# A planner of instruction order with new costs for the opening, new landing times and a new table of noises

## The chip, the cores and the metric

The kernel runs on one core of one Trainium2 chip. The metric is the device time of one execution in microseconds (us). Before the change the median of three runs is 1648.17 us (1646.45 to 1650.07).

## What is computed

The reference has two parts. For each of 8 batches and 8 heads, with 576 positions of 64 elements in float32:

```
kv  = k^T v                      # 64 x 64 per head
out = q kv                       # 576 x 64 per head
x   = out / sqrt(mean(out^2) + 1e-6) * g_norm
```

The heads of a batch are laid side by side, which gives x as 4608 rows of 512. Then four experts, each with weights w1 (512 x 1024) and w2 (1024 x 512):

```
p    = domain_probs / sum(domain_probs)
out += p[:, e] * (relu(x @ w1[e]) @ w2[e])    # for e = 0..3
```

## The kernel before

**Tiling and stages.** x is kept transposed and cut into 9 chunks of 512 rows (the first 512 positions of each batch, and a ninth of what is left over). A step is one expert on one chunk, so there are 36 steps, expert by expert. A step forms the products of x with w1 (`up`), applies relu, and forms the products with w2 (`down` or `down_deep`), one step later. Most products are made by a scheme of seven products of quarter blocks in place of eight, nested twice, so that sums and differences of blocks (`combine`, L549, on DVE or POOL) and evacuations of PSUM (L1417 and L1745 on ACT, L1425 and L1753 on DVE) run beside PE all the time. PE's products of both stages have the line of one helper, L526.

**The opening** (`opening`, from L845) treats batch 0, four pairs of heads. For each pair SP issues the loads of q, k and v (L555). PE turns q (L875, evacuated by ACT, L880), forms keys times values and turns the rest of q (L890, L894), and ACT and DVE copy the result (L909, L906). Two attention products follow (L929), into two halves (`raw`) of shared PSUM banks. Their squares (L805, ACT), sums (L812, DVE), roots (L772) and inverses (L779 to L784), and the scaling (L824, DVE) give x, which PE turns again (L949) and ACT evacuates (L955). Then the first products with w1 (`up_plain`, L526) can run. The remainder of batch 0 is L969 and L983. While PE has nothing to do in the opening, the planner inserts filler products on the identity (L1906).

**The other batches** (`attention`, from L1005) come one per step in steps 0 to 6: q is loaded in eight pieces and transposed by DVE (L1050); products at L1077, L1102, L1144; roots go by DRAM (L1180, L1189, L1196).

**At the expert changes** (steps 8, 17 and 26 on) `weights_1` and `weights_2` load the next weights. Differences with weights that are in DRAM are made by `subtract_from`: ACT writes the negated copy (L622), then POOL issues a load that adds to it (L628). Results of expert 0 go out by SP (L1592), later ones by POOL with addition (L1590), those of the very last step by SP again.

**What sets the order.** The order of the instructions of all five queues is written out when the kernel is built. Each operation is added to a `Plan` with a key (its place in the stream of steps), a cost per engine, and for transfers its size `kb` and the time `lands` from issue to landing. `prepare` gives each a due time: the summed PE cost ahead of its key, lowered so that what depends on it can be on time. `run` then steps through time, and each free engine begins the operation with the earliest due time among those that it takes to be ready (`ready`, `delay`); SP takes the first in order of key. `begin` books the end: for SP a bus of 215 KB per us before `OPEN` = 36 us and 260 after, with at least `lands` after that; for POOL's transfers a bus of 130. Each engine executes its queue in the order so found, and waits for what is really late. `deal` moves the due times of the operations of a step (and of the next) by a pseudorandom noise; the table `DEALS` says which noise each step gets.

The choice in `run` and the landing in `begin`:

```
best = op
if eng in self.FIRST or eng == "PE" and t < self.OPEN:
    break
...
self.bus = max(self.bus, t + 1.5) + op.kb / (215.0 if t < self.OPEN else self.RATE)
op.end = self.bus + 0.5
if t >= self.OPEN:
    op.end = max(op.end, t + op.lands)
```

Of the kernel before, what the change touches and what calls it, by code (L numbers as in the profile page):

```python
# [41 lines left out]
class Plan:  # L42
# [25 lines left out]
    DEALS = {  # L68
        -2: 8, -1: 32, 0: 171, 1: 147, 2: 82, 3: 196, 4: 105, 5: 75, 6: 79, 7: 39, 8: 54, 9: 73, 10: 115,
        11: 84, 12: 12, 13: 6, 14: 6, 16: 1, 17: 3, 18: 10, 19: 11, 20: 2, 21: 1, 22: 4, 23: 4, 25: 5, 26:  # L70
        8, 27: 6, 33: 3, 34: 4
# [33 lines left out]
    def prepare(self, slots, later, idle, idle_banks, idle_until):  # L105
# [49 lines left out]
        self.bus, self.port, self.held, self.bus_pool = 3.8, 0.0, None, 0.0  # L155
# [11 lines left out]
    @staticmethod  # L167
    def noise(*key):

        def mix(x):  # L170
            x = (x ^ x >> 16) * 0x7feb352d & 0xffffffff
            x = (x ^ x >> 15) * 0x846ca68b & 0xffffffff
            return x ^ x >> 16

        n, step, i = key
        x = mix(n * 2654435761 + (step + 8) * 40503 & 0xffffffff)
        x = mix(x + i * 2246822519 & 0xffffffff)
        y = mix(x + 1 & 0xffffffff)
# [3 lines left out]
    def deal(self, step, n):  # L182

        k = len(self.SPREADS)
        wide = self.SPREADS[n % k] if n else 0.0
        wide_pe = self.SPREADS_PE[n // k % len(self.SPREADS_PE)] if n else 0.0
        for op in self.steps[step] + self.steps.get(step + 1, []):
            z = wide_pe if "PE" in op.cost else wide
            op.due = op.base + (z * self.noise(n, step, op.n) if z else 0.0)

    def layout(self, *how):

        self.prepare(*how)
        for step in sorted(self.steps):
            self.deal(step, self.DEALS.get(step, 0))
# [17 lines left out]
    def delay(self, d, eng):  # L213

        if self.t < self.OPEN:
            return 0.06 if d.eng == eng else 0.2
# [8 lines left out]
    def ready(self, op, eng, front):  # L225
# [34 lines left out]
    def run(self, until):  # L260
# [3 lines left out]
        while self.left:  # L264
# [6 lines left out]
            for eng in todo:  # L271
# [10 lines left out]
                for op in pending:  # L282
# [19 lines left out]
                    if eng in self.FIRST or eng == "PE" and t < self.OPEN:  # L302
                        break
# [27 lines left out]
    def begin(self, op, eng):  # L331
        t, wake, free = self.t, self.wake, self.free
        op.start, op.eng = t, eng
        if eng == "SP":
# [3 lines left out]
            if t >= self.OPEN:  # L338
                op.end = max(op.end, t + op.lands)
            self.lanes = self.lanes[1:] + [op.end]  # L340
        else:
            op.end = t + op.cost[eng]
            self.busy[eng] = op.end - (self.OVERLAP[eng] if t >= self.OPEN else 0.0)
            if op.kb:
                self.bus_pool = max(self.bus_pool, op.end + 2.0) + op.kb / self.RATE_POOL
                op.end = max(op.end + op.lands, self.bus_pool)
        if eng == "PE":
            self.worked += op.cost[eng]
        if op.port:
# [20 lines left out]
        for b in op.bufs:  # L370
            b.left -= 1
            if b.left == 0 and b.kind is not None:
                early = t < self.OPEN
                end = max(
                    o.end + (0.2 if early else self.AFTER_PE if o.eng == "PE" else self.FREED)
# [12 lines left out]
        if t < self.OPEN:  # L388
            heapq.heappush(wake, op.end + 0.06)
            heapq.heappush(wake, op.end + 0.2)  # L390
# [11 lines left out]
def kernel(  # L402
# [150 lines left out]
    def load(key, buf, dst, src, kb, reads=(), also=(), lands=4.0, issue=0.55):  # L553
# [64 lines left out]
    def subtract_from(key, to, view, a, src, reads, writes):  # L618
# [10 lines left out]
            reads=[to], writes=writes, kb=512, lands=6.0,  # L629
        )  # L630

    def weights_1(e, key, step, need):
# [4 lines left out]
        for i, (n, dh, uh) in enumerate(((1, 0, 0), (2, 1, 0), (21, 0, 1), (4, 1, 1))):  # L637
# [5 lines left out]
                w1_src(e, dh, uh), 512 if e else 300, also=[corner[n]], lands=6.0,  # L643
# [48 lines left out]
    def weights_2(e, key, step, deep):  # L692
# [3 lines left out]
        for i, (n, uh, dh) in enumerate(((1, 0, 0), (2, 1, 0), (12, 0, 1), (3, 1, 1))):  # L696
# [4 lines left out]
                w2_src(e, uh, dh), 512 if e else 330, also=[corner[n]], lands=6.0,  # L701
# [67 lines left out]
    def inverse_root(key, ss, rt, n, count):  # L769
# [17 lines left out]
        plan.add(key - 0.3, {"ACT": 0.2}, root, reads=[ss], writes=[rt])  # L787
        plan.add(key - 0.3, {"DVE": 0.75}, invert, reads=[ss, rt], writes=[ss, rt], port=True)
# [56 lines left out]
    def opening(key, span, rem):  # L845
# [11 lines left out]
        for hp in range(NPAIR):  # L857
            n = f"{b}_{hp}"
            loaded = {}
            for t, src, kb in (("q", q, 172), ("k", k, 172), ("v", v, 172)):  # L860
# [16 lines left out]
            plan.add(at(hp), {"PE": 0.44}, turns, reads=[qt], writes=[bank])  # L877
# [22 lines left out]
            for other in range(2):  # L900
                to, at_ = (kv_own, kv_other)[other], slice(other * D, (other + 1) * D)
                for r in range(2):
                    c = r ^ other
                    plan.add(
                        at(hp), {"DVE": 0.235} if r else {"ACT": 0.24},
# [17 lines left out]
            def attend(eng, raw=raw, kv=kv, qT=qT, other=0, wide=wide):  # L923
# [12 lines left out]
                at(hp + 0.4), {"PE": 0.36 if wide == D else 0.5}, attend, reads=[qT, kv_own], holds=[kv], writes=[raw])  # L936
            plan.add(
                at(hp + 0.4), {"PE": 0.36 if wide == D else 0.5}, lambda eng, attend=attend: attend(eng, other=1),
# [12 lines left out]
            plan.add(at(hp + 1), pe(4, P, 1), turn_x, reads=[x], writes=[bank])  # L951
# [13 lines left out]
        def attend_rem(eng):  # L965
# [9 lines left out]
            at(NPAIR), {"PE": 0.9}, attend_rem,  # L975
# [29 lines left out]
    def attention(b, key, span, rem):  # L1005
# [26 lines left out]
        for s in range(2):  # L1032
# [3 lines left out]
            for r in range(2):  # L1036
                for dh in range(2):
                    for o in range(2):
# [6 lines left out]
                                "(n p) d -> p n d", p=R), 170 if b == 1 else 118,  # L1045
# [475 lines left out]
    def result(s, e, c, base):  # L1521
# [60 lines left out]
        def send(key, i):  # L1582
# [4 lines left out]
            def fn(eng):  # L1587
# [9 lines left out]
                lands=5.6 if e and not again else 4.5,  # L1597
# [245 lines left out]
    plan.add(-1.99, {"PE": 0.3}, turn_gains, reads=[gain_row], writes=[gain_bank])  # L1843
# [117 lines left out]
```

## Time and profile before

| | |
|---|---|
| median of three runs | 1648.17 us |
| the profiled execution | 1651.69 us |
| its span, first to last instruction | 1649.9 us |
| PE busy, share of the span | 1632.6 us, 99% |
| DVE, ACT, POOL busy | 1316.6, 972.8, 620.5 us |
| granted TensorE clock, mean | 0.999 |
| DMA over the span | 240.97 MB, mean 146 GB/s |

The profile shows one execution. Rows of the time line give the start and the busy us, engine, line, operation, tiles written and read, and how many instructions were merged into the row; the brackets hold the time that the engine was idle before it, and what released it. Lines are those of the kernel before. A matmul in float32 is two instructions in the counts. SPq and POOLq are the queues' own work of issuing transfers. `big`, `u`, `db`, `ab` and so on are kinds of buffers; the last three are banks of PSUM.

### The profile page before, as it was taken

What the parts mean: (1) busy time and instruction counts of PE and PEld (TensorE: products, weight loads), DVE (VectorE), ACT (ScalarE), POOL (GpSimd) and SP (SyncE); (2) the same over time, 40 slices, a digit from 0 to 9 for tenths busy, and PEclk for the clock granted to TensorE, in tenths of its full rate; (3) what the DMA queues carried; (4) which work ended last, traced back from release to release, by engine and by line L of the source; (5) the groups of instructions that cost most, each with busy time, mean ns of one, the idle gap of its engine ahead of it and who ended that gap; (6) DMA issues with size and microseconds to landing.
All of it is one profiled execution on the core that took longest, in us unless ns stands there. A gap on an engine that the chain in (4) does not pass through costs nothing.

```text
span 1649.9 us, 66218 instructions
## 1 busy us (share of the span) xinstructions
PE 1632.6 (99%) x28724; PEld 1554.8 (94%) x28724; DVE 1316.6 (80%) x2188; ACT 972.8 (59%) x2462; POOL 620.5 (38%) x641
## 2 busy tenths in 40 slices
PE   9999999999999999999999999999999999999998
PEld 6688789888999999999999999999999999999997
DVE  5777887878888878788887898777898887778776
ACT  3455554655656666666656666655666566666653
POOL 4132323232433453443344443333344444442333
PEclk9999999999999999999999999999999999999999
DMA  9977886654764435444566444444578444444432
GB/s 230 215 172 206 228 227 174 152 194 175 219 170 130 117 92 155 117 112 109 168 158 167 115 106 119 114 117 113 135 186 187 117 117 117 107 115 116 117 104 53
DMA packets 225597, 240.97 MB, mean 146 GB/s; under 512 B 100890, under 2 KB 165274, under 8 KB 225306
## 3 DMA queue, kind: packets, MB, share of 16 engines
q1 hardware_dynamic: 201690, 199.96, 40.0%
q0 software_dynamic: 23616, 36.78, 14.8%
q8 instruction: 225, 3.69, 0.9%
q14 instruction: 66, 0.54, 0.1%
HBM read 162.21 MB, written 74.47 MB: 143 GB/s over the span
## 4 chain that ended last, share of the span: by engine, by line
PE 92%; DMA 4%; SPq 2%; DVE 1%; issue 1%; ACT 0%; POOL 0%; DVEq 0%; POOLq 0%; ACTq 0%
PE u L526 45%; PE db L526 29%; PE ab L526 15%; DMA out_dram<-big 1%; SPq L555 1%; PE ab L1077 1%; DMA big<-in_moe_w_dram 1%; DMA kv<-in_v_dram 1%; PE ab L1102 1%; DVE big L549 0%; PE ab L1144 0%; DMA big<-roots 0%; PE db L1102 0%; PE ab L1906 0%; PE u L890 0%
## 5 line engine op out<-in xcount | busy, mean ns | idle before, releaser
L549 DVE TENSOR_TENSOR big<-big,big 128x1024 f32<-128x1024 f32 (+1 forms) x539 | 502.0, 946 | 44.8 <-ACT big L1381 18.0
L526 PE MATMUL u<-xf,big 128*64 128x128 f32 x6496 | 476.0, 273 | 0.3
L526 PE MATMUL db<-big,big 128*64 128x128 f32 (+1 forms) x5552 | 425.7, 290 | 1.5 <-ACT big L1745 0.9
L526 PE MATMUL u<-xf,w1y 128*64 128x128 f32 x5304 | 396.5, 273 | 3.8 <-ACT u L1417 2.4
L526 PEld LDWEIGHTS u<-xf,big 128*64 128x64 f32 x6496 | 382.4, 137 | 5.1 <-ACT snap L1417 1.4
L526 PEld LDWEIGHTS db<-big,big 128*64 128x64 f32 x5552 | 332.1, 137 | 28.9 <-ACT big L1745 1.4
L526 PEld LDWEIGHTS u<-xf,w1y 128*64 128x64 f32 x5304 | 314.1, 137 | 8.1 <-ACT u L1417 2.6
L1425 DVE TENSOR_TENSOR big<-u,snap 128x256 f32<-128x256 f32 x448 | 188.3, 421 | 121.2 <-PE u L526 83.7
L1417 ACT ACTIVATE snap<-u 128x256 f32<-128x256 f32 x490 | 187.9, 384 | 148.7 <-PE u L526 130.3
L549 POOL TENSOR_TENSOR big<-big,big 128x256 f32<-128x256 f32 (+1 forms) x145 | 152.7, 1055 | 219.2 <-DVE big L549 111.3
L1417 ACT ACTIVATE big<-u 128x256 f32<-128x256 f32 x448 | 171.1, 385 | 86.9 <-PE u L526 68.0
L549 POOL TENSOR_TENSOR big<-big 128x512 f32<-128x512 f32 (+1 forms) x89 | 107.3, 1207 | 250.7 <-DVE big L549 115.6
L1745 ACT ACTIVATE snap<-db 128x256 f32<-128x256 f32 (+1 forms) x256 | 90.4, 353 | 122.8 <-PE db L526 100.7
L1381 ACT ACTIVATE big<-big 128x1024 f32<-128x1024 f32 x127 | 133.7, 1054 | 12.3 <-DVE big L549 11.2
L1753 DVE TENSOR_TENSOR big<-ab,snap 128x256 f32<-128x256 f32 x174 | 73.2, 421 | 64.4 <-ACT snap L1745 42.6
L1590 POOL DMA_DIRECT2D out_dram<-big x122 | 106.7, 1233 | 31.9 <-ACT big L1566 24.2
L1417 ACT ACTIVATE u<-u 128x256 f32<-128x256 f32 x245 | 90.8, 371 | 37.6 <-PE u L526 25.1
L549 DVE TENSOR_TENSOR big<-big 128x512 f32<-128x512 f32 (+1 forms) x145 | 109.0, 755 | 1.6 <-ACT big L1381 1.5
L526 PE MATMUL ab<-kv,big 128*64 128x128 f32 x1416 | 99.6, 273 | 0.0
L1566 ACT ACTIVATE big<-big,p_all 128x256 f32<-128x256 f32 x200 | 94.1, 503 | 1.6 <-POOL big L1784 0.7
L526 PE MATMUL ab<-big,big 128*64 128x128 f32 (+1 forms) x1304 | 91.3, 274 | 0.0
L1784 POOL TENSOR_TENSOR big<-big 128x512 f32<-128x512 f32 x25 | 31.9, 1274 | 145.1 <-DVE big L549 125.3
(216 smaller groups left out, 2325.5 us busy)
## 6 DMA issues: line engine op xcount, KB each, us to landing
xf<-x SPq DMA_DIRECT2D x104, 512.0 KB, 3.6
xf<-x_h SPq DMA_DIRECT2D x85, 256.0 KB, 3.1
xf<-x SPq DMA_DIRECT2D x78, 256.0 KB, 3.4
out_dram<-big POOLq DMA_DIRECT2D x74, 256.0 KB, 6.5
x<-xf SPq DMA_DIRECT2D x36, 512.0 KB, 5.0
big<-in_moe_w_dram SPq DMA_DIRECT2D x31, 512.0 KB, 5.7
x_h<-big SPq DMA_DIRECT2D x18, 512.0 KB, 4.6
out_dram<-big SPq DMA_DIRECT2D x32, 256.0 KB, 2.8
```

What stands on the lines that cost most here:

```text
L526: nc.tensor.matmul(out_[cols], lhsT=lhsT[:, cols], rhs=rhs, **kw)
L549: lambda eng: adder(eng).tensor_tensor(out=out_(), in0=a(), in1=b(), op=op),
L555: key, {"SP": issue}, lambda eng: nc.sync.dma_start(out=dst(), in_=src), reads=reads,
L1077: nc.tensor.matmul(bank.ap[o * D:(o + 1) * D, r * D:(r + 1) * D], lhsT=ks[r], rhs=vs[r], start=(j == r == 0), stop=(j == len(sets[0]) - 1) ...
L1381: lambda eng: nc.scalar.activation(out=b.ap[:], in_=b.ap[:], func=ACT.Relu),
L1417: lambda eng: nc.scalar.activation(out=where(), in_=ps.ap[:, 0:HN], func=ACT.Copy),
L1425: lambda eng: nc.vector.tensor_tensor(out=block(whole, a, t), in0=src.ap[:, 0:HN], in1=add_.ap[:], op=ALU.add),
L1566: lambda eng: nc.scalar.activation(out=cell(i, half), in_=ap(), func=ACT.Copy, scale=prob()),
L1590: nc.gpsimd.dma_start(out=dst, in_=cell(i)[parts, :], accum_op=ALU.add)
L1745: lambda eng: nc.scalar.activation(out=where(), in_=group_of(ps.ap), func=ACT.Copy),
L1753: lambda eng: nc.vector.tensor_tensor(out=cell(tq, dq), in0=group_of(src.ap), in1=group_of(add_.ap), op=ALU.add,),
L1784: lambda eng: adder(eng).tensor_tensor(out=whole(to), in0=whole(a), in1=whole(b), op=ALU.add),
```

## The change

All of it is in what the planner believes and in the table; no operation is added or left out, and the code that emits instructions is the same. The numbers of instructions can differ only by the fillers. The parts:

1. **Opening.** The separate rules for times before 36 us go: the delays between engines, the overlap, the time until a buffer is free and the turn at the shared port are those of later times, and PE chooses by due time there as well. The bus starts at 2.2 in place of 3.8, the sizes of the opening's loads become one per load, a PE operation before `SLOW` = 6.5 (6.8 before) takes up to twice its cost.
2. **Halves.** A PE operation with a half bank waits, in the plan, until all earlier readers of halves are done, and a reader until all earlier PE writers are done (`seen`, `filled`).
3. **Landings.** `lands` of plain loads 4.0 to 4.6, of weights 6.0 to 6.7, of accumulating weight loads 6.0 to 8.2, of accumulating stores 5.6 to 6.3. A factor `MARGIN` on them stands at 1.0.
4. **Costs** of some operations of the opening, of the root and its inverse; the size of batch 1's q pieces (170 to 120).
5. **Noises.** A step now gets a list of noises, added up; of a noise all, a fifth or a twentieth of the operations are moved (`SHARES`). The table is new throughout.

The diff, cut:

```diff
+        self.halves = any(b.kind == "raw" for b in self.bufs)
...
-    SLOW = 6.8
-    SPREADS = 1.0, 2.0, 4.0
-    SPREADS_PE = 0.0, 0.5, 1.5
-    RATE, RATE_POOL, OPEN = 260.0, 130.0, 36.0
+    SLOW = 6.5
+    SPREADS, SPREADS_PE, SHARES = (1.0, 2.0, 4.0), (0.0, 0.5, 1.5), (1.0, 0.2, 0.05)
+    RATE, RATE_POOL, OPEN, MARGIN = 260.0, 130.0, 36.0, 1.0
     FIRST = "SP",
     DEALS = {
-        -2: 8, -1: 32, 0: 171, 1: 147, 2: 82, 3: 196, 4: 105, 5: 75, 6: 79, 7: 39, 8: 54, 9: 73, 10: 115,
...
+        -3: (61,), -2: (96, 339), -1: (17, 340), 0: (41, 337, 607, 846, 1010), 1: (145, 260, 617, 782,
+        1257), 2: (232, 295, 739, 836), 3: (178, 338, 551, 793, 1009), 4: (138, 447, 504, 966, 1073), 5:
...
-        self.bus, self.port, self.held, self.bus_pool = 3.8, 0.0, None, 0.0
+        self.bus, self.port, self.held, self.bus_pool = 2.2, 0.0, None, 0.0
+        self.seen = self.filled = 0.0
...
+    def chosen(self, n, step, i):
+        return self.mix(self.draw(n, step, i) + 7 & 0xffffffff) / 4294967296.0
...
+    def deal(self, step, draws):
+
+        k, kp = len(self.SPREADS), len(self.SPREADS_PE)
         for op in self.steps[step] + self.steps.get(step + 1, []):
-            z = wide_pe if "PE" in op.cost else wide
-            op.due = op.base + (z * self.noise(n, step, op.n) if z else 0.0)
+            op.due = op.base
+            for n in draws:
+                spread = self.SPREADS_PE[n // k % kp] if "PE" in op.cost else self.SPREADS[n % k]
+                share = self.SHARES[n // (k * kp) % len(self.SHARES)]
+                if spread and self.chosen(n, step, op.n) < share:
+                    op.due += spread * self.noise(n, step, op.n)
...
-        if self.t < self.OPEN:
-            return 0.06 if d.eng == eng else 0.2
...
+        if op.halves:
+            when = max(
+                when, self.seen + self.TO_PE if eng == "PE" else self.filled + self.AFTER_PE)
         if op.port:
-            turn = 0.0 if eng == self.held or self.t < self.OPEN else self.TURN[eng]
+            turn = 0.0 if eng == self.held else self.TURN[eng]
...
-                    if eng in self.FIRST or eng == "PE" and t < self.OPEN:
+                    if eng in self.FIRST:
                         break
...
-                op.end = max(op.end, t + op.lands)
+                op.end = max(op.end, t + op.lands * self.MARGIN)
...
-            self.busy[eng] = op.end - (self.OVERLAP[eng] if t >= self.OPEN else 0.0)
+            if eng == "PE" and t < self.SLOW:
+                op.end += min(op.cost[eng], (self.SLOW - t) / 2)
+            self.busy[eng] = op.end - self.OVERLAP[eng]
...
+        if op.halves and eng == "PE":
+            self.filled = max(self.filled, op.end)
+        elif op.halves:
+            self.seen = max(self.seen, op.end)
...
-    def load(key, buf, dst, src, kb, reads=(), also=(), lands=4.0, issue=0.55):
+    def load(key, buf, dst, src, kb, reads=(), also=(), lands=4.6, issue=0.55):
...
-            reads=[to], writes=writes, kb=512, lands=6.0,
+            reads=[to], writes=writes, kb=512, lands=8.2,
...
-                w1_src(e, dh, uh), 512 if e else 300, also=[corner[n]], lands=6.0,
+                w1_src(e, dh, uh), 512 if e else (300, 300, 344, 450)[i], also=[corner[n]], lands=6.7,
...
-            for t, src, kb in (("q", q, 172), ("k", k, 172), ("v", v, 172)):
+            for t, src, kb in zip("qkv", (q, k, v), (
+                    (172, 194, 290), (183, 150, 150), (237, 400, 150), (172, 150, 172))[hp]):
...
-            plan.add(at(hp), {"PE": 0.44}, turns, reads=[qt], writes=[bank])
+            plan.add(at(hp), {"PE": 0.54}, turns, reads=[qt], writes=[bank])
...
-                lands=5.6 if e and not again else 4.5,
+                lands=6.3 if e and not again else 4.5,
```

More of the change, by code (lines that the diff above doesn't have):

```diff
@@ L700, in weights_2 @@
                 lambda n=n: f[n].ap[:].rearrange("p (k d) -> p k d", k=4),
-                w2_src(e, uh, dh), 512 if e else 330, also=[corner[n]], lands=6.0,
+                w2_src(e, uh, dh), 512 if e else 330, also=[corner[n]], lands=6.7,
             )
@@ L785, in invert @@
                 out=r, in0=w, scalar=1.5, in1=r, op0=ALU.add, op1=ALU.mult)
-        plan.add(key - 0.3, {"ACT": 0.2}, root, reads=[ss], writes=[rt])
-        plan.add(key - 0.3, {"DVE": 0.75}, invert, reads=[ss, rt], writes=[ss, rt], port=True)
+        plan.add(key - 0.3, {"ACT": 0.29}, root, reads=[ss], writes=[rt])
+        plan.add(key - 0.3, {"DVE": 0.81}, invert, reads=[ss, rt], writes=[ss, rt], port=True)
     def scaled(key, name, raw, n, x, blocks, by_half=False):
@@ L904, in opening @@
                     plan.add(
-                        at(hp), {"DVE": 0.235} if r else {"ACT": 0.24},
+                        at(hp), {"DVE": 0.23} if r else {"ACT": 0.22},
                         lambda eng, r=r, c=c, at_=at_, kbank=kbank, kv=kv: nc.vector.tensor_copy(
@@ L949, in turn_x @@
                     nc.tensor.transpose(bank.ap[:, rs], x.ap[:, rs], ident[:])
-            plan.add(at(hp + 1), pe(4, P, 1), turn_x, reads=[x], writes=[bank])
+            plan.add(at(hp + 1), {"PE": 0.64}, turn_x, reads=[x], writes=[bank])
             xh = x_halves(b)[hp // 2]
```

45 lines of the change are left out of this document (18 added, 27 removed), and 4 rows, old and new, of the table DEALS.

## The prediction

> **What bounds the kernel now.** I read the summary of the page first, then the table of stages, then the PE rows that have an idle time, and last what those rows waited for. The profiled execution took 1651.69 us; its span is 1649.9 us, so 1.8 us lie around the span.
>
> ```profile
> span 1649.9 us, 66218 instructions
> ```
>
> The next view gives the busy time of each engine by stage: start and end of the stage, its length, then for each engine the busy us with the number of instructions, the granted clock, the DMA share and GB/s. Only stages with an idle PE are shown, and the sum of all.
>
> ```profile
> 0.00:10.00 10.00, 8.63 (x176) 7.81 (x178) 0.67 (x4) 3.11 (x7) 0.99 (x9) 1.00 0.82 282
> 10.00:20.00 10.00, 9.17 (x194) 7.33 (x188) 6.55 (x23) 6.56 (x22) 4.36 (x6) 1.00 0.99 313
> ...
> 50.00:100.00 50.00, 47.94 (x706) 36.70 (x704) 37.79 (x74) 24.70 (x65) 12.12 (x13) 1.00 0.86 215
> 100.00:200.00 100.00, 97.31 (x1626) 82.18 (x1624) 74.93 (x129) 53.90 (x137) 29.58 (x31) 1.00 0.77 200
> ...
> 400.00:500.00 100.00, 97.61 (x1758) 97.32 (x1756) 84.58 (x149) 59.69 (x146) 38.18 (x43) 0.98 0.61 179
> ...
> 800.00:900.00 100.00, 96.86 (x1756) 95.45 (x1753) 82.74 (x143) 61.94 (x157) 46.37 (x45) 1.00 0.70 176
> ...
> 1600.00:1650.00 50.00, 45.46 (x704) 40.18 (x698) 31.22 (x53) 18.86 (x49) 13.01 (x13) 0.99 0.21 44
> sum 1650.00, PE 1632.59 PEld 1554.76 DVE 1316.61 ACT 972.80 POOL 620.49; mean PE 74.21 PEld 70.67 DVE 59.85 ACT 44.22 POOL 28.20
> ```
>
> PE is the bound: it is idle for 17.4 us of 1650. The reader sees where: 1.4 and 0.8 us in the first 20 us, 2.1 and 2.7 us while the heads of later batches are computed (50 to 200), 2.4 us at 400 to 500, 3.1 us at 800 to 900, 4.5 us in the last stage, and 0.4 us (what is left of the sum) elsewhere. The edit changes no product, so only those idle times, PE's filler products, and time at a low clock can move. All else is PE work that stays: **the most that can be won is about 1%**, and an order can lose more than that.
>
> **The opening, part by part.** The rows are PE's own: start, us, line, operation, count, and in brackets the idle time before.
>
> ```profile
> 1.37 4.10 PE L1906 MATMUL ab<-ident 64*64 64x64 f32 x72 [1.37 <-POOL ident masks.py:199]
> 5.41 1.11 PE L875 MATMUL ab<-ident,big 128*128 128x128 f32 x4
> 6.45 1.07 PE L1906 MATMUL ab<-ident 64*64 64x64 f32 x24
> 7.36 1.21 PE L890 MATMUL u<-big,big 64*64 64x64 f32 x36
> ...
> 10.04 1.23 PE L890 MATMUL u<-big,big 64*64 64x64 f32 x36
> ...
> 12.00 1.35 PE L890 MATMUL u<-big,big 64*64 64x64 f32 x36
> ...
> 13.51 0.69 PE L929 MATMUL db<-kv,big 64*64 64x64 f32 x32
> ...
> 15.33 0.66 PE L949 MATMUL ab<-ident,big 128*128 128x128 f32 x4 [0.54 <-DVE big L824]
> ...
> 18.68 3.65 PE L526 MATMUL u<-big,big 128*64 128x512 f32 x16 [0.23 <-issue]
> ```
>
> L1906 is filler, 8 instructions a piece: the planner puts one in when it believes that nothing is ready. The first 72 and the 24 at 6.45 (1.07 us) stand ahead of the first product of keys and values at 7.36. Were its operands there? The issue rows of SP, and for each of those issues the time from its start to its landing (last number):
>
> ```profile
> 0.76 0.40 SPq L555 DMA_DIRECT2D big<-in_q_dram  x1
> 1.67 0.43 SPq L555 DMA_DIRECT2D big<-in_v_dram  x1
> 4.81 0.58 SPq L555 DMA_DIRECT2D big<-in_v_dram  x1
> ```
>
> ```profile
> big<-in_q_dram SPq DMA_DIRECT2D x1, 288.0 KB, 2.8
> ```
>
> ```profile
> big<-in_v_dram SPq DMA_DIRECT2D x1, 288.0 KB, 4.1
> ```
>
> ```profile
> big<-in_v_dram SPq DMA_DIRECT2D x1, 288.0 KB, 7.0
> ```
>
> The first q lands at 0.76 + 2.8 = 3.6 us, and PE turns it only at 5.41: 1.8 us late. The first v lands at 1.67 + 4.1 = 5.8 us, and its product runs at 7.36: 1.6 us late. The old planner starts its bus at 3.8 us and so believes in late first landings; the edit starts it at 2.2 with sizes per load: q at 2.2 + 172/215 + 0.5 = 3.5, v after 172 + 194 + 290 at 2.2 + 656/215 + 0.5 = 5.75. Both agree with the rows. So some four fillers go (of the 12), the turn of q moves to about 3.7, and the product to about 6.1, a filler's length (1.07/3 = 0.36) being lost in the rounding: **1.2 to 1.6 us earlier.** What is late next: the third v, at 4.81 + 7.0 = 11.8 us, whose product runs at 12.00 and can't come earlier. Between the two there is then 1.3 us of PE time to fill; one attention product (0.69, now at 13.51) fits there, since the second keys-and-values product that it needs, now at 10.04, moves ahead too; about 0.6 us may stay empty. On top of that, the gaps at 15.33 and 18.68 (0.54 + 0.23) are for the taking: the first waits for a scaling on DVE, and that is where the two halves of a bank count: one `raw` half is written while the other is read, which the planner did not know. So: 1.3 - 0.6 = 0.7 at least, 1.3 + 0.8 = 2.1 at best, **I take 1.4 us**. That the opening loses is bounded by the same 0.8: PE now picks by due time, not by the first in key order, and a second gap of the size of these two would cost it.
>
> **The expert changes.** PE rows with the two largest late stalls, then ACT's rows that stand at their root, then the chain of waits at the two places (start, us, what).
>
> ```profile
> 488.20 1.12 PE L526 MATMUL u<-xf,w1y 128*64 128x128 f32 x8 [2.39 <-ACT u L1417]
> 863.58 0.66 PE L526 MATMUL u<-xf,w1y 128*64 128x128 f32 x8 [0.89 <-DVE small L1425]
> 881.47 0.66 PE L526 MATMUL u<-xf,small 128*64 128x128 f32 x8 [2.17 <-ACT snap L1417]
> ```
>
> ```profile
> 486.82 1.06 ACT L622 ACTIVATE big<-big 128x1024 f32<-128x1024 f32 x1 [3.64 <-DMA out_dram<-big]
> ```
>
> ```profile
> 880.09 1.06 ACT L622 ACTIVATE big<-big 128x1024 f32<-128x1024 f32 x1 [2.55 <-DMA big<-in_moe_w_dram]
> ```
>
> ```profile
> 476.65 10.09 DMA out_dram<-big
> ```
>
> ```profile
> 868.74 11.33 DMA big<-in_moe_w_dram
> ```
>
> Both are one pattern: the negated copy of weights (L622) sits in ACT's queue, waits for a landing, and the copies of products (L1417) behind it, for which PE waits, can't pass. The edit raises the planned landing of the accumulating weight load from 6.0 to 8.2 us, and that of the accumulating store on POOL's queue from 5.6 to 6.3. For the stall at 881 that is 2.2 us more patience against 2.17 of idle PE: I count it gone, as the copy will be placed behind other ACT work. The one at 863 waits for DVE behind such a store: 0.7 of its 0.89 goes. Together **2.9 us**. The one at 488 stays in my sum at nothing: its landing is a plain store issued by SP, planned at 4.5 us before and after, and it took 10.09. The ends are: all of them gone, and none with new ones beside (the slower rival).
>
> A stall can cost more than itself, by the granted clock:
>
> ```profile
> 480.00:490.00 10.00, 7.61 (x126) 7.37 (x122) 5.77 (x13) 4.80 (x11) 3.98 (x5) 0.91 0.95 265
> 490.00:500.00 10.00, 10.00 (x172) 10.00 (x170) 8.91 (x12) 5.52 (x13) 3.54 (x5) 0.92 0.60 120
> ```
>
> 10 x (0.09 + 0.08) = 1.7 us of full-speed PE is lost after the 2.39 us of idle, though the 2.17 us at 881 lost none (clock 1.00 in that stage). [...]
>
> **The attention steps, 50 to 200 us.** One example, SP's issues, then DVE, then PE:
>
> ```profile
> 71.17 7.82 SPq L555 DMA_DIRECT2D small<-in_q_dram  x8
> ```
>
> ```profile
> 81.25 1.38 DVE L1050 STREAM_TRANSPOSE small<-small 128x1152 f32<-128x1152 f32 x1 [2.48 <-DMA small<-in_q_dram]
> ```
>
> ```profile
> 82.99 0.66 PE L526 MATMUL u<-big,w1y 128*64 128x128 f32 x8 [1.72 <-DVE big L1425]
> ```
>
> A transposition of q waits in DVE's queue 2.48 us for its load, with the sum of products (L1425) that PE needs behind it. The planner counts 8 x 0.68 = 5.4 us for those eight issues, and they took 7.8; the edit leaves that number alone. So no corrected constant mends this stall: only the choice of the noises can, since the new table is one under which late landings were tried too. Ends: none of the 2.1 + 2.7 + 0.4 = 5.2 us is won, or all of it. No row is nearer to the one than to the other, so I take the middle, **2.6 us**. The other end, below nothing: a table for a new order can make as many of these waits again, 5.2 us lost. The first 1.37 us (building the identity) and the last stage's 4.5 us stay; the products' and the roots' new costs only describe, at nothing.
>
> **The sum** is 1.4 + 2.9 + 2.6 = 6.9 us. The profiled execution (1651.69) lies 3.52 us above the median of the three (1648.17); these stalls hang on landings and will differ by execution, so part of that 3.52 is the stalls themselves, already absent from the median. I start from the middle of the two, 1649.9: **1649.9 - 6.9 = 1643.0 us.**
>
> **The rivals.** (a) *The stalls are dealt anew.* The table is new at every step, so the place of each copy in its queue is new; the late landings stay as they are, and as much PE time is lost elsewhere. For it: the plain stores, the q issues and the roots keep their constants. Against it: the stages from 200 to 400, 500 to 800 and 900 to 1600 us hold 0.4 us of idle PE in all, so orders nearly without stalls exist. Only the opening's 1.4 is left: 1648.5. (b) *The opening's gain is swallowed.* PE is ready earlier, but the DMA share is 0.99 in the second 10 us and 0.86 up to 100; if loads are the bound there, PE waits 1.4 us longer behind 50 us: 1649.9 - 2.9 - 2.6 = 1644.4. (c) *All stalls go*, by luck and a good choice: 1649.9 - 2.1 - (0.89 + 2.17 + 2.39 + 1.7) - 5.2 = 1635.5; the part of that in the median is gone already, so about 1639. (d) *Slower: one more copy in ACT's queue ahead of a late landing.* Where L622 waited 3.64 us, PE idled 2.39: PE had 3.64 - 2.39 = 1.25 us of ready products. Here is the point from which it decides: a landing later than the plan by more than 1.25 us beyond the planned slack. The rows for it are these medians, which the new constants are close to, while single landings took 10.09 and 11.33:
>
> ```profile
> out_dram<-big POOLq DMA_DIRECT2D x74, 256.0 KB, 6.5
> ...
> out_dram<-big SPq DMA_DIRECT2D x32, 256.0 KB, 2.8
> ```
>
> ```profile
> big<-in_moe_w_dram POOLq DMA_DIRECT2D x16, 512.0 KB, 8.6
> ```
>
> So a constant per kind of transfer can't hold them; with several noises the copy is moved in more ways. At 2.39 + 1.7 = 4.1 us for one new stall, and only the opening won: 1649.9 - 1.4 + 4.1 = 1652.6, slower by 0.27%. [...]
>
> **How the numbers follow.** A measurement of this kernel tells about 0.2% (3.3 us) from no change: faster is below 1644.9, slower above 1651.5. The forecast has 0.50, of which 0.10 ends within 0.2%; (a) has 0.17 and ends there; (b) 0.04 and (c) 0.08 are faster; (d) has 0.21. So faster 0.40 + 0.04 + 0.08 = 0.52, within 0.10 + 0.17 = 0.27, slower 0.21. The range goes from (c), 1639, to just below (d), 1652, with about one in ten outside at either end.
>
> **What would show it.** Opening: fewer than 96 instructions at L1906 before the first L890, that L890 near 6.1 instead of 7.36, no gap over 0.3 us before the L526 products, and these starting near 17.3 instead of 18.68. Expert changes: no wait of ACT at L622 above 1 us near 880, no DVE wait for a POOL store near 860; that near 488 may stay. Attention: idle PE of 50 to 200 us near half of 4.8. It is wrong if the first L890 is not earlier, if idle PE from 20 to 1600 us is above 9 us, or if a granted clock below 1.00 shows in more than one place.

## The result and the profile after

The changed kernel takes 1639.58 us (median of 6 runs, 1637.57 to 1644.63); the kernel before took 1649.12 us in the same measurement (6 runs, 1646.45 to 1651.61). The ratio is 0.9945, with a 95% interval of 0.9927 to 0.9962: faster by 0.4 to 0.7%. The forecast was 1643.0, within 1639 to 1652. The profiled execution took 1638.29 us.

The page of the kernel after has this span:

```profile
span 1636.5 us, 66139 instructions
```

It is 13.4 us shorter than the 1649.9 of before. Where did they come from? The same four stages of both kernels (start and end, length, busy us of each engine with its count, clock, DMA share, GB/s), first of the kernel before:

```profile
0.00:50.00 50.00, 47.79 (x608) 28.82 (x608) 27.61 (x75) 21.37 (x59) 17.71 (x27) 1.00 0.97 240
50.00:400.00 350.00, 344.87 (x5600) 293.33 (x5598) 269.77 (x477) 189.57 (x477) 103.70 (x121) 1.00 0.72 195
400.00:1000.00 600.00, 594.47 (x10836) 592.61 (x10834) 500.20 (x829) 370.45 (x934) 256.61 (x257) 1.00 0.52 138
```

and of the kernel after:

```profile
0.00:50.00 50.00, 47.59 (x622) 27.89 (x624) 29.76 (x77) 23.72 (x65) 16.91 (x26) 1.00 1.00 246
50.00:400.00 350.00, 349.35 (x5684) 303.22 (x5682) 273.46 (x491) 191.04 (x481) 112.36 (x116) 1.00 0.71 195
400.00:1000.00 600.00, 597.90 (x10942) 596.86 (x10940) 507.16 (x841) 373.17 (x940) 255.09 (x248) 1.00 0.53 140
```

Length less the first busy number is PE's idle time. In the attention steps (50 to 400) it falls from 5.1 to 0.65 us, at the expert changes (400 to 1000) from 5.5 to 2.1, in the opening not at all (2.2 and 2.4), though 1.2 us of filler has gone there. From 1000 to 1600 neither has any, and the ends are about alike. That is 4.5 + 3.4 + 1.2 - 0.2. The kernel before also lost 1.7 us to a low clock at 490 us, and the kernel after does not (1.00 from 480 to 500): 10.6 of the 13.4. Idle time can't show the rest, since the row of one matmul is 273 ns long (mean of L540 on the page of after) while one follows another each 55 ns (16 at 839.25 us of after move PE on by 0.87 us), so shorter gaps are counted as busy. The products themselves give an estimate without that fault. Both kernels have the same ones (28,724 matmul instructions with 96 fillers, and 28,692 with 64). By 50 us the kernel after has done 48 short ones more (L1159 and L1165, 1.13 us in a row) and two of 0.23 us fewer, so it is 0.7 us ahead. From 50 to 400 us it does 132 of 55 ns more, 7.2 us, of which those 0.7 are to be taken: 6.5. From 400 to 1000 us it does 106 more: 5.8. With 0.4 us less idle time in the last stage that is the 13.4.

These parts hold for the two executions that were profiled. The one of before lies 2.6 us above its median and the one of after 1.3 below, so the parts add to 3.9 us more than the 9.5 by which the medians differ.

The opening after, on PE; the rows answer to those of before, complete up to the third product of keys and values (L905 is the old L890, L890 the old L875, L944 the old L929, L1921 the filler):

```profile
1.37 2.40 PE L1921 MATMUL ab<-ident 64*64 64x64 f32 x40 [1.37 <-POOL ident masks.py:199]
3.71 1.12 PE L890 MATMUL ab<-ident,big 128*128 128x128 f32 x4
4.76 1.55 PE L1921 MATMUL ab<-ident 64*64 64x64 f32 x24
6.10 1.39 PE L905 MATMUL u<-big,big 64*64 64x64 f32 x36
7.42 0.30 PE L909 MATMUL u<-ident,big 128*64 128x128 f32 x1
7.66 0.28 PE L1855 MATMUL u<-ident,p_all 1*64 1x1 f32 x4
7.87 0.66 PE L890 MATMUL ab<-ident,big 128*128 128x128 f32 x4
8.45 0.69 PE L944 MATMUL db<-kv,big 64*64 64x64 f32 x32
8.96 1.23 PE L905 MATMUL u<-big,big 64*64 64x64 f32 x36
10.13 0.30 PE L909 MATMUL u<-ident,big 128*64 128x128 f32 x1
10.26 0.60 PE L890 MATMUL ab<-ident,big 128*128 128x128 f32 x4
10.79 0.80 PE L944 MATMUL db<-kv,big 64*64 64x64 f32 x32
11.41 0.28 PE L905 MATMUL u<-big,big 64*64 64x64 f32 x3
12.72 1.15 PE L905 MATMUL u<-big,big 64*64 64x64 f32 x33 [1.03 <-issue]
...
16.13 1.08 PE L540 MATMUL u<-big,big 128*64 128x512 f32 x4
```

The first q is turned at 3.71 (5.41 before), the first product is at 6.10 (7.36), the second attention product (10.79) has moved ahead of the third product, and the gaps at 15 and 18 us are gone. New is a hole of 1.03 us ahead of 12.72, in the middle of a product, three matmul instructions after its start; the last section has what the traces show of it.

The one large late stall after, on PE, then ACT's row at its root, then the chain of waits:

```profile
857.08 1.09 PE L540 MATMUL db<-kv,big 128*64 128x128 f32 x16 [2.10 <-ACT ab L1760]
```

```profile
855.42 1.06 ACT L636 ACTIVATE big<-big 128x1024 f32<-128x1024 f32 x1 [2.64 <-DMA big<-in_moe_w_dram]
```

```profile
844.73 10.67 DMA big<-in_moe_w_dram
```

It is the pattern of before: the negated copy (L636, the old L622) waits in ACT's queue, and the evacuations behind it can't pass.

### The profile page after: what moved, and what is told of

It is laid out like the page before. It is cut to its first block, busy times and chain, and to the rows that moved or that the text cites. A ratio compares the mean times of both kernels' runs of the same rounds, so it can differ in the third digit from the quotient of the medians.

```text
span 1636.5 us, 66139 instructions
## 1 busy us (share of the span) xinstructions
PE 1627.3 (99%) x28692; PEld 1555.0 (95%) x28692; DVE 1317.3 (80%) x2211; ACT 971.9 (59%) x2462; POOL 625.7 (38%) x618
## 4 chain that ended last, share of the span: by engine, by line
PE 97%; DMA 1%; DVE 1%; SPq 0%; issue 0%; ACT 0%; POOL 0%; DVEq 0%; POOLq 0%; ACTq 0%
PE u L540 47%; PE db L540 31%; PE ab L540 15%; PE ab L1092 1%; DMA big<-in_moe_w_dram 1%; PE ab L1117 1%; PE ab L1159 0%; PE db L1117 0%; DMA big<-roots 0%; SPq L569 0%; PE u L905 0%; PE ab L1921 0%; PE db L944 0%; DVE xf L563 0%; DMA small<-in_q_dram 0%
## 5 line engine op out<-in xcount | busy, mean ns | idle before, releaser
L563 DVE TENSOR_TENSOR big<-big,big 128x256 f32<-128x256 f32 (+1 forms) x522 | 478.2, 932 | 28.1 <-ACT big L1396 13.6
L540 PE MATMUL u<-xf,big 128*64 128x128 f32 x6784 | 493.8, 273 | 0.0
L540 PE MATMUL db<-big,big 128*64 128x128 f32 (+1 forms) x5648 | 434.0, 290 | 0.4 <-DVE big L563 0.4
L540 PEld LDWEIGHTS u<-xf,big 128*64 128x64 f32 x6784 | 398.7, 137 | 2.9 <-issue 0.8
L540 PE MATMUL u<-xf,w1y 128*64 128x128 f32 x5304 | 395.4, 273 | 0.1
L540 PEld LDWEIGHTS db<-big,big 128*64 128x64 f32 x5648 | 339.8, 137 | 25.3 <-DVE big L563 0.9
L540 PEld LDWEIGHTS u<-xf,w1y 128*64 128x64 f32 x5304 | 313.5, 137 | 5.1 <-issue 1.0
L563 POOL TENSOR_TENSOR big<-big,big 128x256 f32<-128x256 f32 (+1 forms) x162 | 187.4, 1158 | 255.6 <-DVE big L563 110.6
L563 DVE TENSOR_TENSOR big<-big 128x512 f32<-128x512 f32 (+1 forms) x160 | 122.3, 772 | 2.4 <-PE db L540 1.2
L1605 POOL DMA_DIRECT2D out_dram<-big x104 | 93.8, 1229 | 36.5 <-ACT big L1581 23.1
L540 PE MATMUL ab<-kv,big 128*64 128x128 f32 x1504 | 104.6, 273 | 0.0
L540 PE MATMUL ab<-big,big 128*64 128x128 f32 (+1 forms) x1384 | 96.9, 275 | 0.0
L540 PEld LDWEIGHTS ab<-kv,big 128*64 128x64 f32 x1504 | 87.2, 137 | 0.0
L540 PEld LDWEIGHTS ab<-big,big 128*64 128x64 f32 x1384 | 80.5, 137 | 1.2
```

Of the source, the lines that this page charges most:

```text
L540: nc.tensor.matmul(out_[cols], lhsT=lhsT[:, cols], rhs=rhs, **kw)
L563: lambda eng: adder(eng).tensor_tensor(out=out_(), in0=a(), in1=b(), op=op),
L1605: nc.gpsimd.dma_start(out=dst, in_=cell(i)[parts, :], accum_op=ALU.add)
```

## The experiments

Each run is compared with the kernel before on the same chip. Since that kernel's own median moved between the three groups (1649.24, 1650.62, 1649.97), I set ratios beside ratios. Theory and rivals at the start: the constants mend the opening and the expert changes and the choice of noises the attention steps (theory); the table does all behind the opening (first rival); any order is as good as another, and the old one was a bad draw (second rival).

**old_plain.** The kernel before, `DEALS = {}`.

> The kernel before with an empty table: its own costs and landings, no noise at any step. Theory (constants mend the opening and the expert changes, the choice of noises mends the attention steps): the old table was worth something too, so this is slower than before by 2 to 8 us (1651 to 1657), with idle PE between 50 and 400 us above 5.1. Rival (any order is as good as another, the gain was luck in the draw): within 3 us of before.

**new_plain.** The kernel after, `DEALS = {}`.

> The kernel after with an empty table: only the new costs, landings and halves. Theory: the constants alone bring 1.4 (opening) + 2.9 (expert changes), so this is 4.3 us better than the old planner without noises, and slower than the kernel after (1639.6) by at least the 2.6 of the attention steps. Rival (the table does all of it): no more than 1.4 us better than the old planner without noises. Rival (luck): about 1640.

Measured: old_plain 1674.34 us, ratio 1.0164 (1.0146 to 1.0182); new_plain 1666.83, 1.0114 (1.0098 to 1.0130). Stages of old_plain:

```profile
50.00:400.00 350.00, 330.27 (x5226) 276.33 (x5226) 250.07 (x440) 180.99 (x444) 92.71 (x104) 1.00 0.66 173
400.00:1000.00 600.00, 598.60 (x10842) 593.13 (x10840) 516.91 (x847) 368.60 (x931) 264.62 (x257) 1.00 0.56 147
```

and of new_plain:

```profile
0.00:50.00 50.00, 45.17 (x570) 26.20 (x572) 25.10 (x67) 21.82 (x61) 19.93 (x28) 1.00 0.99 244
50.00:400.00 350.00, 335.04 (x5274) 280.23 (x5272) 259.63 (x456) 180.75 (x446) 77.93 (x97) 1.00 0.65 174
400.00:1000.00 600.00, 599.07 (x10888) 594.47 (x10886) 523.38 (x855) 370.37 (x939) 246.32 (x253) 1.00 0.56 147
```

Both expectations were far too small: without a table either planner loses 25 to 27 us against its own. Nearly all of it goes in the attention steps, where 374 and 410 fewer matmul instructions are done between 50 and 400 us, some 20 and 22 us at 55 ns each; idle PE there is 19.7 and 15.0 us, which is 14.6 and 14.3 more than with the tables, and the rest is again in gaps that count as busy. The two differ by 7.5 us, so the first rival's 1.4 is wrong as well. The difference lies in the attention steps (4.8 us of idle PE), where I had priced the constants at nothing. But each is one order, and other orders differ there by as much (open_new below), so that the constants themselves are worth it is not shown. And the last row of old_plain says something about the kernel before: **with the old landings and no noise the stages from 400 to 1000 us hold 1.4 us of idle PE, not 5.5.** The stalls at 488, 863 and 881 came with the order that the old table chose; the old landings alone don't make them.

**new_redealt.** The kernel after; from step 1 on each number of the table raised by 1350 (4050 at step 6), which keeps width and share:

```diff
-        1257), 2: (232, 295, 739, 836), 3: (178, 338, 551, 793, 1009), 4: (138, 447, 504, 966, 1073), 5:
+        2607), 2: (1582, 1645, 2089, 2186), 3: (1528, 1688, 1901, 2143, 2359), 4: (1488, 1797, 1854,
```

> The kernel after with the chosen noises up to step 0, and from step 1 on as many noises of the same widths and shares whose numbers nobody chose (each number raised by 1350, or 4050 at step 6). Theory: the choice is worth the 2.6 us of the attention steps, so 1642 to 1643, with the expert changes no worse. Rival (the table does all after the opening): 1647.7 or more. Rival (luck in the draw): 1639.6 within 2 us.

Measured: 1650.37 us, ratio 1.0003 (0.9994 to 1.0012). The attention steps:

```profile
50.00:400.00 350.00, 343.99 (x5520) 293.51 (x5522) 266.84 (x489) 186.55 (x469) 91.39 (x99) 1.00 0.73 194
```

6.0 us of idle PE where the chosen table has 0.65. With unchosen noises **the whole gain is gone**: 0.0058 in the ratio, some 9.6 us. The theory's 2.6 fell, the second rival (luck) too; the first rival holds in size. This is one draw of unchosen noises. It is still 16.5 us faster than new_plain, which has none, though that run lacks the chosen noises of the opening as well: most of what a table brings came here without choosing.

**open_new.** The kernel after with the landings of before and with the old table from step 1 on; new are only the opening's constants, rules and entries.

```diff
-    def load(key, buf, dst, src, kb, reads=(), also=(), lands=4.6, issue=0.55):
+    def load(key, buf, dst, src, kb, reads=(), also=(), lands=4.0, issue=0.55):
...
-                share = self.SHARES[n // (k * kp) % len(self.SHARES)]
+                share = 1.0 if step in self.FULL else self.SHARES[n // (k * kp) % len(self.SHARES)]
```

> The opening's part alone: new bus, sizes, costs, delays and halves and the new table up to step 0; old landings and the old table from step 1 on. Theory: the first product of keys and values starts near 6.1 us, fillers 64, and 0.7 to 2.1 us of the time are won: 1647.0 to 1648.4 from 1649.1, unless the stalls behind move. Rival (the gain is swallowed by loads): 1649.1, with the opening's rows as early but idle PE from 50 to 100 us larger by 1.4.

Measured: 1658.08 us, ratio 1.0057 (1.0044 to 1.0071), slower by more than either theory said. The opening is as early as after's, but behind it:

```profile
12.49 1.15 PE L899 MATMUL u<-big,big 64*64 64x64 f32 x33 [1.15 <-issue]
```

```profile
50.00:400.00 350.00, 338.78 (x5478) 289.27 (x5476) 261.10 (x472) 184.66 (x464) 97.62 (x106) 1.00 0.70 189
```

11.2 us of idle PE, against 5.1 with the old opening in front of the same table. In this run the table was worth less behind a state for which it was not chosen; so the parts of this change don't add up, and the opening's part can't be measured alone in this way.

After this the theory was: the chosen noises clear the attention steps, and the constants give them a better start; what the landings do at the expert changes is open.

**one_noise.** The kernel after; from step 1 on only the first noise of each list.

> The kernel after with the opening's lists as they are (up to step 0) and from step 1 on only the first noise of each list. Theory, as it stands now (the choice of several noises per step clears the attention steps, the constants do little there): some of the idle PE of 50 to 400 us comes back, 1 to 5 us slower than after, so 1640.6 to 1645. Rival (one well-chosen noise does as much, the constants made the difference): within 1 us of after, 1639.6.

Measured: 1641.51 us, ratio 0.9948 (0.9933 to 0.9963), against 0.9945: not told apart. In the attention steps the trace does:

```profile
50.00:400.00 350.00, 347.66 (x5656) 299.20 (x5655) 268.69 (x503) 191.65 (x480) 111.69 (x104) 1.00 0.71 194
```

2.3 us of idle PE against 0.65. The first noise of a list brings most (the unchosen ones left 6.0), the others perhaps 1.7 more, read from one trace of each; the times don't resolve it.

**old_pool_landings.** The kernel after with `lands` 8.2 back to 6.0 (accumulating weight loads) and 6.3 back to 5.6 (accumulating stores). The order is the same up to step 7.

> The kernel after with the two landings of POOL's transfers as before (8.2 back to 6.0, 6.3 back to 5.6). Up to step 7 the order is the same; from the first expert change on it differs. Theory of the prediction (longer planned landings keep the negated copy from blocking ACT): the waits of ACT for such landings return at 450 to 550 and 830 to 900 us, 2 to 4 us slower than after. Rival (a landing that is late by 4 us and more isn't held by these constants, the places fall anew): within 2 us of after either way, with stalls at other places.

Measured: 1644.19 us, ratio 0.9964 (0.9953 to 0.9976). Its late stages:

```profile
400.00:1000.00 600.00, 597.24 (x10898) 594.28 (x10896) 508.86 (x834) 372.98 (x937) 264.86 (x251) 1.00 0.54 140
1000.00:1600.00 600.00, 598.73 (x10961) 597.94 (x10958) 481.88 (x756) 369.88 (x944) 228.94 (x222) 1.00 0.50 124
```

The ratio is 0.0019 above that of after, some 3.1 us and the theory's size, but the two intervals overlap, so the times alone don't part it from nothing. The stage from 400 to 1000 has the stall of after again (2.42 us at 860), behind a plain weight load. New is the one past 1200; ACT's row at its root, then the chain of waits:

```profile
1250.68 1.06 ACT L636 ACTIVATE big<-big 128x1024 f32<-128x1024 f32 x1 [1.84 <-DMA big<-in_moe_w_dram]
```

```profile
1237.91 12.66 DMA big<-in_moe_w_dram
```

That transfer was issued by POOL: one stall of the theory's kind did return, for the 1.27 us that the stage lacks, at another place than those of before. It is less than half of the 3.1, so both theories may have a part.

**late_plain** and **late_plain_old_pool** take the table away there: the kernel after with `DEALS` up to step 7 only, and the same with 6.0 and 5.6.

> The kernel after with no noises from step 8 on; up to step 7 the order is the same. Theory (the new landings mend the expert changes by themselves): no more than 1 us slower than after, idle PE from 400 to 950 us at most 3 us. Rival (the table does all after the opening): 3 us slower or more, 1642.6 up, the idle PE in the same stages.

> As late_plain, with the two landings of POOL's transfers as before (6.0 and 5.6), so that no table is tuned to either. Theory (the longer planned landings are worth some 2.9 us by themselves): 2 to 4 us slower than late_plain. Rival (what old_pool_landings lost by them was the tuning of the table, not the landings): within 1 us of late_plain.

Measured, in one group: late_plain 1638.56 us, 0.9939 (0.9923 to 0.9956); late_plain_old_pool 1640.43, 0.9949 (0.9933 to 0.9965). Stage 400 to 1000 of the first, then of the second:

```profile
400.00:1000.00 600.00, 598.66 (x10932) 596.19 (x10930) 515.49 (x837) 371.28 (x939) 259.50 (x250) 1.00 0.55 140
```

```profile
400.00:1000.00 600.00, 598.84 (x10920) 595.30 (x10917) 515.01 (x833) 372.44 (x939) 271.20 (x254) 1.00 0.55 140
```

From step 8 on the table is worth nothing that can be measured. The longer planned landings differ by 1.9 us, between the theory's 2 to 4 and the rival's 1, and these intervals separate it neither from none nor from the theory. Idle PE is 1.3 and 1.2 us. But the waits of ACT behind POOL's loads do return in the second run, and the first has none:

```profile
492.69 1.06 ACT L629 ACTIVATE big<-big 128x1024 f32<-128x1024 f32 x1 [1.50 <-DMA big<-in_moe_w_dram]
875.21 1.06 ACT L629 ACTIVATE small<-big 128x1024 f32<-128x1024 f32 x1 [1.24 <-DMA big<-in_moe_w_dram]
```

PE has other products during both: it has no idle time from 485 to 500 us nor from 870 to 880. **Neither the new landings nor noises are needed for a quiet expert change; the stalls of before came with the old table.** Under a table the landings do matter, as the stall at 1250 in old_pool_landings shows; whether that table was only no longer fitting, as in open_new, can't be told from it.

**patience_weights.** The kernel after, plain weight loads of expert 2 alone:

```diff
-                w2_src(e, uh, dh), 512 if e else 330, also=[corner[n]], lands=6.7,
+                w2_src(e, uh, dh), 512 if e else 330, also=[corner[n]], lands=11.0 if e == 2 else 6.7,
```

and the same for w1.

> The kernel after with the planned landing of the plain weight loads of expert 2 at 11.0 in place of 6.7; the order up to step 16 is the same. After had one large stall left: ACT's negated copy waited for such a load, which took 10.67 us, and PE idled 2.10 us. Theory (a copy in ACT's queue blocks when its landing is later than planned): the copy goes behind other work, the 2.1 us go, 1637.5 or a little less. Rival (the stall comes from the shortage of buffers, or moves to the next landing): no faster than after, with a stall of 1 us or more between 820 and 900 us.

Measured: 1636.17 us, ratio 0.9918 (0.9902 to 0.9934), **the best of all**, lower than the kernel after by 0.0027 in the ratio (its interval overlaps by 0.0007 with that of after). No idle PE is left there:

```profile
400.00:1000.00 600.00, 600.00 (x10990) 599.49 (x10988) 508.81 (x844) 376.05 (x944) 256.60 (x248) 1.00 0.54 141
```

The load at that place was no quicker than before. It takes 10.5 us and lands at 855.51, and the copy now begins behind it without a wait (the load, from its issue at 844.97; then ACT's row):

```profile
big<-in_moe_w_dram SPq DMA_DIRECT2D x1, 512.0 KB, 10.5
```

```profile
856.91 1.05 ACT L636 ACTIVATE big<-big 128x1024 f32<-128x1024 f32 x1
```

So the mechanism of the prediction's slower rival is shown by its cure: the copy was put behind other work, and the stall went.

**patience_all.** The same for the loads of experts 1, 2 and 3.

> As patience_weights, with 11.0 for the weight loads of experts 1, 2 and 3; the order up to step 7 is the same as after's. Theory (only a copy that really met a late landing gains): the one wait for a load at 490 us (1.61 us of ACT, no idle PE) goes, no gain beyond patience_weights: 1636 within 1 us. Rival (any change behind step 8 upsets the table): slower than patience_weights by 2 us or more.

Measured: 1636.65 us, ratio 0.9923 (0.9908 to 0.9938), the time that the theory gave. Its reason doesn't hold: the wait at 490 us was for a load of POOL (11.23 us in the kernel after), whose planned landing this run leaves alone. It is 0.29 us here and 0.69 in patience_weights, whose order is that of after up to there, so it shrank without the change.

**no_filler.** The kernel after without fillers (`idle_until` -99).

> The kernel after without filler products; PE's real work in the opening is planned at almost the same times. [...] Rival (they only fill): 1639.6 within 0.5. Rival (they delay the first product, as 24 of them stood before it in the kernel before): faster by up to 0.4 us.

Measured: 1640.42 us, ratio 0.9940 (0.9924 to 0.9957): no difference in time that can be told. In the rows there is one:

```profile
3.84 1.08 PE L890 MATMUL ab<-ident,big 128*128 128x128 f32 x4 [3.84 <-DMA big<-in_q_dram]
5.60 2.19 PE L905 MATMUL u<-big,big 64*64 64x64 f32 x36 [0.67 <-DMA big<-in_v_dram]
...
10.33 1.98 PE L905 MATMUL u<-big,big 64*64 64x64 f32 x36
...
13.42 1.23 PE L905 MATMUL u<-big,big 64*64 64x64 f32 x36
```

The same 36 matmuls take 2.19, 1.98 and then 1.23 us: without fillers the slow speed lasts to some 12 us, and the third product begins at 13.42, where the larger part of after's begins at 12.72. Whether this reaches the total can't be told: the interval is 0.0017 to either side, 2.7 us. The execution that was profiled met the stall at 857 us again, 2.87 us long, and there the granted clock read 0.98 from 800 to 900 us, some 2 us of PE lost by that mean, and 0.90 from 860 to 870; the 2.10 us of after cost no clock (1.00 from 850 to 870).

**late_start.** The kernel after with all orders kept, and three fillers more ahead of the first product (`for _ in range(3): idle(spare)` behind the first turn of q).

> The kernel after, all orders as they are, with three more fillers ahead of the first product of keys and values, which then starts near 7.2 us, as in the kernel before (7.36). Theory as it stands now (the earlier start was swallowed by the wait of 1.03 us for the third v at 12.7 us, and the opening won by its missing gaps behind): that wait shrinks to nearly nothing, the products at L540 start as early, time within 0.5 us of after (1639.6). Rival (my forecast: the earlier start carries through): the wait stays at 0.6 or more, all is later by 0.7 to 1.1 us, 1640.5.

Measured: 1637.79 us, ratio 0.9937 (0.9920 to 0.9954), no slower than after. Its rows:

```profile
6.68 1.21 PE L905 MATMUL u<-big,big 64*64 64x64 f32 x36
...
12.28 0.51 PE L944 MATMUL db<-kv,big 64*64 64x64 f32 x18 [0.64 <-issue]
...
15.33 1.33 PE L944 MATMUL db<-kv,big 64*128 64x64 f32 x16 [0.39 <-ACT rt L786]
...
17.17 1.08 PE L540 MATMUL u<-big,big 128*64 128x512 f32 x4
```

The first product is 0.58 us later than after's, the first at L540 1.04 us later: the rows speak for carrying through, against the theory of then, and the total against it. An effect of 1 us is below what these runs resolve, so it stays open.

## Why the prediction was right, point by point

**The bound** was right as far as idle time shows it: 10.6 of the 13.4 us are idle PE, fillers and clock, and the products add gaps too short to see. The sum was 6.9 us from 1649.9; the medians moved by 9.5. At 1639.58 the time lies 0.6 us inside the lower end of the range, where rival (c) stood with a chance of 0.08. The three terms had the right sign, but the opening's was sized too high and the other two too low; that the time still fell inside the range is in part luck.

**The opening**: 1.4 us forecast; the trace has 1.2 us less filler and 0.2 more idle, so 1.0, and the products give 0.7: at the lower end of the stated 0.7 to 2.1. No run measures this part alone. The start at 6.1 came to 0.1 us as worked out, the two gaps went, and the attention product moved as said. One sign failed: "no gap over 0.3 us before the L526 products" met the hole of 1.03. One step was wrong in its cause, "the third v, at 4.81 + 7.0 = 11.8 us, whose product runs at 12.00 and can't come earlier". After, that v is issued and lands so (SP's row, then the time to landing):

```profile
4.82 0.52 SPq L569 DMA_DIRECT2D big<-in_v_dram  x1
```

```profile
big<-in_v_dram SPq DMA_DIRECT2D x1, 288.0 KB, 5.9
```

at 4.82 + 5.9 = 10.7 us; its product starts at 11.41 and then stands still for 1.03 us, with its data there. The row names neither a landing nor an engine for that wait (last section), and the prediction has no term for it.

**The expert changes**: 2.9 us forecast, 3.4 us of idle and 1.7 of clock won, 5.8 by the products. The mechanism of a single stall was right (copy, late landing, ACT's queue), as patience_weights shows. The step that failed is the reason given: "For the stall at 881 that is 2.2 us more patience against 2.17 of idle PE: I count it gone". Taking the new landings of POOL's transfers back brings one such stall of PE (1.2 us) under the table; without one it brings two waits of ACT (1.50 and 1.24 us) and no stall of PE behind them; and the old planner without noises has no stall of PE above 0.5 us from 400 to 1000 us. So a longer planned landing does keep ACT from waiting, but what PE loses by such a wait is set by the order around it, and the patience can't be set against the idle PE one for one. The three went, it seems, mostly because the order was drawn anew, as rival (a) has it, only to a good draw; that includes the stall at 488, which I left at nothing.

**The attention steps**: 2.6 us forecast, 4.5 of idle time won, 6.5 by the products. That "only the choice of the noises can" mend them was right in direction: unchosen noises leave 6.0 us idle. Whether the constants mattered as well is open (4.8 us between the two planners without tables, one order each). The example was read too simply. DVE's waits for q in the kernel before, then after:

```profile
DVE small L1050 <- DMA small<-in_q_dram: 5.3, 3, 2.5
```

```profile
DVE small L1065 <- DMA small<-in_q_dram: 4.3, 2, 2.2
```

The waits stayed (5.3 and 4.3 us, the longest 2.5 and 2.2); what changed is that PE now has other products while they last. The middle between none and all of the 5.2 us was the term that was mis-sized.

**The rivals**: (a) names the right lever, the new table, but not that its lots were chosen; (b) did not happen as stated, since idle PE from 50 to 200 us fell from 4.8 to 0.65 us, though the hole in the opening took some of the early start; (c) was nearest in value: 1639 against 1639.6, and patience_weights shows that the late stall could go too; (d) did happen once, at 857, for 2.10 us without loss of clock. At the same place it is 1.28 us in one_noise, 1.39 in late_start and 2.87 with loss of clock in no_filler, so its price differs by run.

## What to carry to other kernels

An order that was searched for is a fit: change a constant ahead of it and the fit is lost (in open_new 9 us, as much as the whole change was worth), so constants and table have to be changed together, and a part can't be judged with the other part's table. Where an in-order engine holds one instruction that waits for a transfer, try to plan that transfer with the latest landing seen, not the median: 11.0 in place of 6.7 for a few loads removed the last 2 us stall here, at no cost that shows. And a wait that stays in the profile is no loss if the bound engine has other work; look at what stands behind it.

## What the runs showed of the hardware that was not expected

**A hole at a place in PE's instruction stream.** Adding up the counts of the rows of after, the hole at 12.72 lies behind 40 + 4 + 24 + 36 + 1 + 4 + 4 + 32 + 36 + 1 + 4 + 32 + 3 = 221 matmul instructions. In all ten kernels with the new opening and the same fillers it is behind the 221st, 0.40 to 1.15 us long, ending between 11.87 and 12.87 us, with no landing and no engine as releaser (`issue` in the bracket). In late_start, with 24 more ahead, it is behind the 222nd and so in another operation (L944, 0.64 us). So in these eleven traces it goes with the count of the instructions (221 or 222), not with the operation. In the kernel before and in old_plain the 221st is the third of the product at 12.00 and 12.03, and the rows show no gap there. All of after's product but its first three matmul instructions comes at 12.72, so the earlier start of PE was not kept up to this place. The DMA engines are full at that time (share 1.06 between 10 and 20 us in the kernel after). What PE waits for in the hole is not shown.

**Slow matmuls that the clock column doesn't show.** In no_filler the first product of keys and values runs at 0.56 of the later speed (1.23 against 2.19 us), and slow products last for some 8 us, from 3.84 to 12 us, while the granted clock reads 1.00 in that stretch. In the kernel after, whose fillers run from 1.37 us on, the first two of these products take 1.39 and 1.23 us. What sets the speed is not shown.
